# V's matmuls directly behind the scores, ahead of the transposes of q and k, in the attention slots of an attention and cosine-gated FFN kernel

## The chip, the cores and the metric

The kernel runs on one core of a Trainium2 chip. The metric is the device time of one execution in microseconds (us); less is better. TensorE does matmuls and transposes, VectorE, ScalarE and GpSimd the elementwise work, and SyncE issues the DMAs. Each engine works through its own queue of instructions; semaphores hold an instruction until what it reads is there or the buffer that it writes is free.

## What is computed

Attention with a bias that a small network makes out of the distance of two positions, and then a feed-forward layer with a cosine gate. Sizes: 4 batches, 8 heads, 576 positions, 64 dimensions a head; 2304 tokens of 512, hidden layer of 2048.

```python
def _attn_ref(q, k, v, w1, b1, w2):
    B, H, S, D = q.shape
    scale = 1.0 / np.sqrt(D)
    scores = scale * np.matmul(q, k.transpose(0, 1, 3, 2))
    ...
    h = np.maximum(x @ w1 + b1, 0.0)
    bias = h @ w2
    scores = scores + bias.transpose(2, 0, 1)[None, :, :, :]
    scores = scores - np.max(scores, axis=-1, keepdims=True)
    attn = np.exp(scores)
    attn = attn / (np.sum(attn, axis=-1, keepdims=True) + 1e-09)
    return np.matmul(attn, v).astype(np.float32)

def _moe_ref(x, w_in, w_out):
    h = x @ w_in
    g = h * np.cos(h)
    return (g @ w_out).astype(np.float32)
```

## The kernel before

Three stages follow one another: the bias tables (to about 65 us), attention (to about 370 us), and the feed-forward layer. The change touches attention alone.

A *unit* is a pair of heads of one batch; there are 16 units. The 576 rows of q are taken in five tiles: four of 128 rows, of two heads each, and a fifth that holds the last 64 rows of both heads. One tile of one unit is a *job*, and each job has a *slot*; a unit has five slots, `j` = 0 to 4, called the first to the fifth slot here. `slot(i)` writes the program out by hand, and the order in which it calls its parts is the order in which each engine gets its instructions; no scheduler moves them. A slot works on several jobs at a time:

- `qk`: the scores of the job now, on TensorE (`s`, L406), and on VectorE the bias and the row minimum (`P` and `m`, L419), which free the scores' bank. There are two buffers for `s`, one per head.
- `softmax_exp`: the exponential of the last job, one per head, on ScalarE (L437), with its sum into `dn`.
- `turn`: the transposes of the next unit's q and k on TensorE (L191, L208), a part in each of the first four slots and none in the fifth (`T_EARLY`), each followed by a copy on ScalarE (`kN`, `qT`, L198; L211 and L213 for the rest).
- `pv`: V's matmuls of the last unit (L524), in four of the five slots (`PV_EARLY`). A half of the rows is done in two slots: in the first slot of each pair chunks 0 and 1 (8 matmul instructions in the trace), in the second chunks 2 to 4 (12), and then ScalarE copies the sum into `xT` (L479, `act_copy`). So the copy into `xT` stands in the second and in the fifth slot.
- `ptrans`, `ptrans_left`: the transposes of P of the job three back (L466, L471), with copies into `PT` by ScalarE for head 0 (L479) and by VectorE for head 1 (L482), and into `PX` by VectorE (L482). All transposes share three banks (`pt`).
- `recip` and `norm`: on VectorE the step on `dn` (L449) and the reciprocal (L452), ahead of that slot's copies into `PT` and `PX`; then the normalisation of P on GpSimd (L459), in whose queue the splits of q and k (L176, L179) stand behind it.

The first slot's V matmuls read what the fifth slot just before put into `PT`; the fourth slot's read what the third put there.

```python
        T_EARLY = [["kh"], ["kl"], ["kx", "qh"], ["ql"], []]
        PV_EARLY = [[(-1, 0, (0, 1))], [(-1, 0, (2, 3, 4))], [], [(-1, 1, (0, 1))], [(-1, 1, (2, 3, 4))]]
```

In slots of every second unit VectorE and ScalarE also widen weights for the next stage (`W_PLAN`, L99 to L107).

Of the kernel before, what the change touches and what calls it, by code (L numbers as in the profile page):

```python
# [28 lines left out]
def kernel(  # L29
# [42 lines left out]
    NU = len(units)  # L72
# [38 lines left out]
    with tc.manual_schedule():  # L111
# [76 lines left out]
        def turn_main(u, x, a):  # L188
            ps = bank(F32R)
            for c in range(4):  # L190
                nc.tensor.transpose(ps[:, 128 * c : 128 * c + 128], spl[u, x][:, a, c], identr)  # L191
            if x == "q":
                o = qTs[u % 2][:, a]
            else:
                if u not in kN:
                    kN[u] = tp.tile([128, 2, 640], F32R, tag="kN", name="kN")
                o = kN[u][:, a, 64:576]
            nc.scalar.activation(  # L198
                out=o.rearrange("p (x c) -> p x c", c=4),
                in_=f(ps).rearrange("p (c x) -> p x c", c=4),  # L200
                func=AF.Copy,
                scale=-0.125 if x == "q" else 1.0,
            )

        def turn_left(u):
            ps = bank(F32R)
            for a in range(2):
                nc.tensor.transpose(ps[:, 128 * a : 128 * a + 128], spl[u, "k"][:, a, 4], identr)  # L208
            i = f(ps)[:, 0:256].rearrange("p (a x) -> p a x", a=2)
            for o in (576, 0):  # L210
                nc.scalar.activation(out=kN[u][:, :, o : o + 64], in_=i[:, :, 0:64], func=AF.Copy)  # L211
            for r in (slice(0, 64), slice(64, 128)):
                nc.scalar.activation(out=qDs[u % 2][r, :, r], in_=i[r, :, 64:128], func=AF.Copy, scale=-0.125)  # L213

        def turn(u, ops):
            if u >= NU:
                return
            for op in ops:
                if op == "kx":
                    turn_left(u)  # L220
                else:
                    turn_main(u, op[0], "hl".index(op[1]))
# [168 lines left out]
        def alloc_half(u, hf):  # L391
            PT[u, hf] = ptp.tile([128, 2, 4, WQ[hf]], F32, tag=f"h{hf}", name=f"PT{hf}")
            PX[u, hf] = px.tile([128, WQ[hf]], F32, tag=f"x{hf}", name=f"PX{hf}")
# [3 lines left out]
        def qk(u, j):  # L397
            t = tiles[j]
            heads = range(2 if t < 4 else 1)
            s = [ps_s.tile([128, 2, 512], F32, tag="s", name="s") for h in heads]  # L400
            for hf in range(2):
                for n, (a, b) in enumerate(((0, 0), (0, 1), (1, 0))):
                    for h in heads:
                        r = slice(64 * h, 64 * h + 64) if t < 4 else slice(0, 128)
                        o = HALF * hf + (64 if h == 0 else 0)
                        nc.tensor.matmul(  # L406
                            s[h][:, hf, 0:HALF],
                            qTs[u % 2][r, a, 128 * t : 128 * t + 128] if t < 4 else qDs[u % 2][:, a],
                            kN[u][r, b, o : o + HALF],
                            start=(n == 0),  # L410
                            stop=(n == 2),
                            tile_position=(r.start, 0),
                        )
            hp = units[u][0]
            P[u, j] = pp.tile([128, 1152], F32, tag="p", name="P")
            for h in heads:
                neg = P[u, j][:, 576 * h : 576 * h + 576]
                m = sv.tile([128, 2], F32, tag=f"m{h}", name="m")
                nc.vector.tensor_tensor_reduce(  # L419
                    neg.rearrange("p (a x) -> p a x", a=2),  # L420
                    s[h][:, :, 0:HALF],
                    bias[hp, t, h].rearrange("p (a x) -> p a x", a=2),
                    1.0,
                    3.0e38,
                    ALU.add,
                    ALU.min,
                    m[:, 0:1],
                )
                cur[u, j, h] = (neg, m)
# [3 lines left out]
        def softmax_exp(u, j, h):  # L433
            neg, m = cur.pop((u, j, h))
            if h == 0:
                dn[u, j] = sv.tile([128, 2], F32, tag="dn", name="dn")
            nc.scalar.activation(  # L437
                out=P[u, j][:, 576 * h : 576 * h + 576],
                in_=neg,
                func=AF.Exp,  # L440
                bias=m[:, 0:1],
                scale=-1.0,
                accum_out=dn[u, j][:, h : h + 1],
            )
# [33 lines left out]
        def act_copy(o, i):  # L478
            nc.scalar.activation(out=o, in_=i, func=AF.Copy)  # L479
# [34 lines left out]
        def pv(u, hf, chunks):  # L514
            hp, b = units[u]
            n = vN[u % 2]
            if 0 in chunks:
                X_[u, hf] = ps_v.tile([128, 512], F32, tag="v", name="pv")
            ps = X_[u, hf]
            for c in chunks:  # L520
                for h in range(2):
                    r = slice(0, 128) if c < 4 else slice(64 * h, 64 * h + 64)
                    a, m = n[r, 4 * h + c if c < 4 else 8], PT[u, hf][:, h, c, :] if c < 4 else PX[u, hf][r]
                    nc.tensor.matmul(  # L524
                        ps[64 * h : 64 * h + 64, 0 : WQ[hf]],
                        a,
                        m,
                        start=(c == 0),
                        stop=(c == 4),
                        tile_position=(r.start, 64 * h),  # L530
                        skip_group_check=True,
                    )
            if 4 in chunks:
                c0 = b * S + 256 * hf
                act_copy(xT[:, hp, c0 : c0 + WQ[hf]], X_.pop((u, hf))[:, 0 : WQ[hf]])
# [10 lines left out]
        PV_EARLY = [[(-1, 0, (0, 1))], [(-1, 0, (2, 3, 4))], [], [(-1, 1, (0, 1))], [(-1, 1, (2, 3, 4))]]  # L546
# [4 lines left out]
        def slot(i):  # L551
            u, j = divmod(i, 5)
            now, last, prev = get(i), get(i - 1), get(i - 3)
            heads = lambda x: range(2 if tiles[x[1]] < 4 else 1)
            if now:
                qk(u, j)
            if last:
                softmax_exp(*last, 0)
            turn(u + 1, T_EARLY[j])
            if last and len(heads(last)) == 2:  # L560
                softmax_exp(*last, 1)
            for du, hf, chunks in PV_EARLY[j]:
                if 0 <= u + du < NU:
                    pv(u + du, hf, chunks)
            if prev:
                if prev[1] in (0, 2):
                    alloc_half(prev[0], prev[1] // 2)
                pt = [ptrans(*prev, h) for h in heads(prev)]
                pl = ptrans_left(*prev)
            if last:  # L570
                recip(*last, 0)
                recip(*last, 1)
            if prev:
                if len(pt) == 2:
                    keep_main(*prev, 0, pt[0])
                    keep_main(*prev, 1, pt[1])
                else:
                    keep_both(prev[0], pt[0])
            if last:
                for h in heads(last):  # L580
                    norm(*last, h)
            if prev:
                keep_left(*prev, pl)
            if now:
                for du, x, step in POOL_PLAN[j]:
                    if u + du < NU:
                        split(u + du, x, step)
                for du, x in LOAD_PLAN[j]:
                    if u + du < NU:
                        load(u + du, x)  # L590
                hp, b = units[u]
                if b == B - 1 and hp + 1 < HP:
                    load_bias(hp + 1, tiles[j])
                if u == NU - 1 and j < KD:
                    split_x(0, 0, j)
                for step, at in W_PLAN:
                    w, r = divmod(i - 0 - at, 10)
                    if r == 0 and 0 <= w < len(wparts):
                        if step == "load":
                            if w + 2 < len(wparts):  # L600
                                load_w(*wparts[w + 2])
                        elif step == "abs":
                            abs_w(*wparts[w])
                        else:
                            widen_w(*wparts[w], step)
# [226 lines left out]
```

## Time and profile before

| | |
|---|---|
| median of 3 runs | 783.94 us (783.48 to 785.31) |
| profiled execution | 785.39 us, of which the profile's span is 783.6 us |
| TensorE busy | 755.1 us, 96% of the span |
| VectorE, ScalarE, GpSimd busy | 599.4, 465.4 and 395.3 us (76%, 59%, 50%) |
| TensorE's mean granted clock | 0.982 of full speed |

Busy shares are means over stages with different limits. Times below are counted from the span's start. A matmul's end is modelled in the profile, and the next one can start before it; where things follow one another without a pause, the distance of two starts is the surer measure.

### The profile page before, as it was taken

To read this page: it belongs to the slowest core of one execution; us is meant where nothing else is said; L and a number is where in the kernel's file an instruction comes from. 1 tells how busy PE (TensorE), PEld (TensorE's weight loads), DVE (VectorE), ACT (ScalarE), POOL (GpSimd) and SP (SyncE) were. 2 spreads that over 40 slices of the span, in tenths; PEclk is the share of its full clock that TensorE was granted. 3 is DMA by queue.
4 is the path that set the end of the run, shared out by engine and by line. 5 is a ranking of instruction groups with operands and counts; after the bars stand their busy time and mean duration, and the time that the engine had idled before them with its cause. 6 is when DMAs were issued, how large, how long until landed. Compare 5 with 4: busy or idle time off the path is not lost.

```text
span 783.6 us, 14808 instructions
## 1 busy us (share of the span) xinstructions
PE 755.1 (96%) x5338; PEld 603.7 (77%) x5338; DVE 599.4 (76%) x1309; ACT 465.4 (59%) x964; POOL 395.3 (50%) x486
## 2 busy tenths in 40 slices
PE   6988899999999999998999999999999999999997
PEld 2665676667666667666798989988888889899895
DVE  8973768687777777775468878899889898976655
ACT  5975677777777777785355555545454545443332
POOL 2201566676767666657345537455455464554400
PEclk9995899999999999999999999999999999999999
DMA  5775314422533161120010101111110101001112
GB/s 184 249 253 188 98 48 135 121 78 56 166 91 89 49 191 49 28 61 11 1 54 28 55 28 54 32 50 31 50 53 30 54 27 55 2 28 41 54 41 81
DMA packets 58825, 58.57 MB, mean 75 GB/s; under 512 B 28544, under 2 KB 45056, under 8 KB 58752
## 3 DMA queue, kind: packets, MB, share of 16 engines
q1 hardware_dynamic: 58752, 57.63, 24.3%
q8 instruction: 42, 0.69, 0.4%
q14 instruction: 31, 0.25, 0.1%
HBM read 42.00 MB, written 15.61 MB: 74 GB/s over the span
## 4 chain that ended last, share of the span: by engine, by line
PE 85%; DVE 6%; DMA 4%; ACT 2%; issue 2%; SPq 0%; DVEq 0%; ACTq 0%
PE ph L634 25%; PE po L689 24%; PE pv L524 12%; PE s L406 9%; PE pt L466 8%; PE pa L323 3%; PE pt L191 3%; DMA sc<-rt 2%; DVE P L419 1%; DVE ht L307 1%; PE pt L471 1%; DMA bt<-sc 1%; DVE PT L482 1%; DVE gl L663 1%; DVE acc L712 0%
## 5 line engine op out<-in xcount | busy, mean ns | idle before, releaser
L459 POOL TENSOR_SCALAR P<-P,rc 128x576 f32<-128x576 f32 x144 | 107.3, 756 | 112.7 <-ACT P L437 40.5
L638 ACT ACTIVATE a<-ph,quarter 128x384 int32<-128x384 f32 x96 | 55.6, 580 | 107.8 <-PE ph L634 107.0
L419 DVE CUSTOM_DVE_ANT_0 P<-s,bt 128x576 f32<-128x576 f32 x144 | 103.5, 751 | 20.6 <-PE s L406 13.7
L644 DVE SCALAR_TENSOR_TENSOR r<-a,ph 128x384 f32<-128x384 int32 x96 | 52.8, 550 | 79.5 <-ACT a L638 79.4
L437 ACT ACTIVATE P<-P,m 128x576 f32<-128x576 f32 x144 | 110.8, 771 | 2.6 <-DVE m L419 2.6
L509 POOL TENSOR_TENSOR xs<-xT,xs 128x384 fp32r<-128x384 f32 x96 | 107.2, 1116 | 8.0
L634 PE MATMUL ph<-xs,wpre 128*128 128x384 f32 x576 | 109.4, 338 | 0.8 <-DVE a L653 0.8
L634 PE MATMUL ph<-xs,w 128*128 128x384 f32 x576 | 108.3, 337 | 0.5 <-DVE a L653 0.5
L634 PEld LDWEIGHTS ph<-xs,wpre 128*128 128x128 f32 x576 | 101.8, 188 | 6.5 <-DVE a L653 2.1
L634 PEld LDWEIGHTS ph<-xs,w 128*128 128x128 f32 x576 | 101.4, 188 | 5.5 <-DVE a L653 1.4
L649 ACT ACTIVATE r<-r,hpi 128x384 f32<-128x384 f32 x96 | 59.3, 617 | 69.6 <-DVE r L645 69.6
L508 POOL TENSOR_SCALAR xs<-xT 128x384 fp32r<-128x384 f32 x96 | 61.6, 641 | 48.7 <-PE ph L634 48.7
L466 PEld LDWEIGHTS pt<-ident,P 128*128 128x128 f32 x576 | 62.9, 143 | 29.7 <-POOL P L459 13.7
L466 PE MATMUL pt<-ident,P 128*128 128x128 f32 x576 | 81.5, 283 | 2.3 <-DVE PT L482 2.3
L524 PE MATMUL pv<-PT,vN 128*64 128x320 f32 (+1 forms) x512 | 77.8, 424 | 2.6 <-ACT PT L479 2.4
L406 PE MATMUL s<-kN,qT 64*128 64x288 f32 x768 | 77.0, 323 | 2.8 <-DVE m L419 1.4
L689 PE MATMUL po<-w,gh 128*128 128x512 f32 x288 | 75.3, 396 | 0.0
L689 PE MATMUL po<-wpre,gh 128*128 128x512 f32 x288 | 75.2, 396 | 0.0
L663 DVE TENSOR_TENSOR gl<-a,gh 128x384 fp32r<-128x384 f32 x96 | 74.0, 771 | 0.6 <-ACT gh L657 0.6
L406 PEld LDWEIGHTS s<-kN,qT 64*128 64x128 f32 x768 | 59.0, 195 | 15.6 <-issue 7.5
L482 DVE COPY PT<-pt 128x512 f32<-128x512 f32 x64 | 43.9, 686 | 33.5 <-PE pt L466 33.5
L109 POOL TENSOR_TENSOR w<-wb,w 128x512 fp32r<-128x512 f32 x16 | 20.7, 1295 | 89.9 <-ACT w L107 89.9
(82 smaller groups left out, 1300.6 us busy)
## 6 DMA issues: line engine op xcount, KB each, us to landing
sc<-rt SPq DMA_DIRECT2D x36, 295.5 KB
raw<-in_moe_w_in_dram SPq DMA_DIRECT2D x16, 512.0 KB
raw<-in_moe_w_out_dram SPq DMA_DIRECT2D x16, 512.0 KB
bt<-sc SPq DMA_DIRECT2D x16, 288.0 KB
nk<-in_k_dram SPq DMA_DIRECT2D x16, 256.0 KB
nq<-in_q_dram SPq DMA_DIRECT2D x16, 256.0 KB
vN<-in_v_dram SPq DMA_DIRECT2D x32, 128.0 KB
bt<-sc SPq DMA_DIRECT2D x16, 256.0 KB
```

The lines of the kernel that those rows point to most:

```text
L406: nc.tensor.matmul(s[h][:, hf, 0:HALF], qTs[u % 2][r, a, 128 * t : 128 * t + 128] if t < 4 else qDs[u % 2][:, a], kN[u][r, b, o : o + HALF ...
L419: nc.vector.tensor_tensor_reduce(neg.rearrange("p (a x) -> p a x", a=2), s[h][:, :, 0:HALF], bias[hp, t, h].rearrange("p (a x) -> p a x", ...
L437: nc.scalar.activation(out=P[u, j][:, 576 * h : 576 * h + 576], in_=neg, func=AF.Exp, bias=m[:, 0:1], scale=-1.0, accum_out=dn[u, j][:, h ...
L459: nc.gpsimd.tensor_scalar(p, p, r, 1.0, ALU.mult, ALU.mult)
L466: nc.tensor.transpose(ps[:, 128 * c : 128 * c + 128], p[:, o : o + 128], ident)
L508: nc.gpsimd.tensor_scalar(h, src, 1.0, 1.0, ALU.mult, ALU.mult)
L509: nc.gpsimd.tensor_tensor(l, src, f(h), ALU.subtract)
L524: nc.tensor.matmul(ps[64 * h : 64 * h + 64, 0 : WQ[hf]], a, m, start=(c == 0), stop=(c == 4), tile_position=(r.start, 64 * h), skip_group_ ...
L634: nc.tensor.matmul(ps, a, x, start=(i == 0), stop=(i == 3 * KD - 1))
L649: nc.scalar.activation(out=r, in_=r, func=AF.Sin, scale=SIN_SCALE, bias=hpi)
L663: nc.vector.tensor_tensor(gl, a, f(G[key][0]), ALU.subtract)
L689: nc.tensor.matmul(O[n][i], a[:, 128 * i : 128 * i + 128], w, start=(i0 == 0 and p == 0), stop=(i0 == GF - 1 and p == 2),)
```

## The change

In `slot` the loop that calls `pv` moves up, from behind the second `softmax_exp` to ahead of `turn`:

```diff
             if last:
                 softmax_exp(*last, 0)
+            for du, hf, chunks in PV_EARLY[j]:
+                if 0 <= u + du < NU:
+                    pv(u + du, hf, chunks)
             turn(u + 1, T_EARLY[j])
             if last and len(heads(last)) == 2:
                 softmax_exp(*last, 1)
-            for du, hf, chunks in PV_EARLY[j]:
-                if 0 <= u + du < NU:
-                    pv(u + du, hf, chunks)
             if prev:
```

On TensorE, the second slot of a unit before (scores, transposes of k, V's matmuls on `PT` and `PX`, transposes of P, the next scores):

```order
L406 MATMUL s<-kN,qT_108 128x288 x12
L191 MATMUL pt<-identr,sk 128x128 x4
L524 MATMUL pv<-PT_1281,vN_115 64x256 x4
L524 MATMUL pv<-PX_1282,vN_115 64x256 x2
L466 MATMUL pt<-ident,P 128x128 x8
L471 MATMUL pt<-ident,P 128x128
```

The same place now:

```order
L406 MATMUL s<-kN,qT_108 128x288 x12
L524 MATMUL pv<-PT_1281,vN_115 64x256 x4
L524 MATMUL pv<-PX_1282,vN_115 64x256 x2
L191 MATMUL pt<-identr,sk 128x128 x4
L466 MATMUL pt<-ident,P 128x128 x8
L471 MATMUL pt<-ident,P 128x128
```

V's six rows of the program (12 in the trace) went ahead of the four transposes of k, which now stand with those of P. On ScalarE, the second slot of a unit, before with - and now with + (L437 is the exponential, `kN` the copy of the transposes of k, `xT` that of V's sum, `PT` that of P's transposes):

```order
 L479 ACTIVATE PT_1377<-pt 128x4x128
 L437 ACTIVATE P,dn<-P,m 128x576
-L198 ACTIVATE kN<-pt 128x512
-L437 ACTIVATE P,dn<-P,m 128x576
-L479 ACTIVATE xT<-pv 128x256
+L479 ACTIVATE xT<-pv 128x256
+L198 ACTIVATE kN<-pt 128x512
+L437 ACTIVATE P,dn<-P,m 128x576
 L479 ACTIVATE PT_1377<-pt 128x4x128
 L437 ACTIVATE P,dn<-P,m 128x576
```

The copy into `xT` went ahead of the copy into `kN` and of head 1's exponential. On ScalarE, the fifth slot, where nothing moves on TensorE:

```order
 L437 ACTIVATE P,dn<-P,m 128x576
 L479 ACTIVATE PT_1555<-pt 128x4x128
-L437 ACTIVATE P,dn<-P,m 128x576 x2
-L479 ACTIVATE xT<-pv 128x320
+L437 ACTIVATE P,dn<-P,m 128x576
+L479 ACTIVATE xT<-pv 128x320
+L437 ACTIVATE P,dn<-P,m 128x576
 L479 ACTIVATE PT_1555<-pt 128x4x128
 L437 ACTIVATE P,dn<-P,m 128x576
```

The copy into `xT` went in between the two exponentials of a job. The orders on VectorE, GpSimd and SyncE are as before.

## Rows read from the trace of the kernel before

**Rows 1.** Busy time by engine, 118 to 350 us; the columns' names first.

```profile
core 0: us, PE busy (x) PEld busy (x) DVE busy (x) ACT busy (x) POOL busy (x), PEclk, DMA share, GB/s
118.00:350.00 232.00, 229.34 (x1938) 160.26 (x1938) 175.66 (x509) 176.81 (x427) 154.90 (x208) 1.00 0.33 93
```

**Rows 2.** Waits from 99 to 372 us: total us, times, longest us.

```profile
ACT xT L479 <- PE pv L524: 18.1, 29, 1.1
...
PEld pt L471 <- ACT qD L213: 5.1, 13, 0.4
...
PEld s L406 <- DVE m L419: 3.6, 8, 1.1
```

**Rows 3.** Timeline of TensorE, last unit: start, duration, engine, line, operation.

```profile
341.69 1.05 PE L406 MATMUL s<-kN,qT 64*128 64x288 f32 x12
342.67 1.08 PE L524 MATMUL pv<-PT,vN 128*64 128x256 f32 x8
```

**Rows 4.** Timeline of TensorE, 264 to 302 us: the unit from 268.25, and the next.

```profile
271.85 1.06 PE L406 MATMUL s<-kN,qT 64*128 64x288 f32 x12
272.84 0.54 PE L191 MATMUL pt<-identr,sk 128*128 128x128 f32 x4
273.31 1.08 PE L524 MATMUL pv<-PT,vN 128*64 128x256 f32 x8
...
274.91 1.09 PE L466 MATMUL pt<-ident,P 128*128 128x128 f32 x8
...
278.62 1.58 PE L406 MATMUL s<-kN,qT 64*128 64x288 f32 x12
...
283.76 1.30 PE L524 MATMUL pv<-PT,vN 128*64 128x320 f32 x8
...
286.80 1.05 PE L406 MATMUL s<-kN,qT 64*128 64x288 f32 x12
...
298.28 0.54 PE L191 MATMUL pt<-identr,sq 128*128 128x128 f32 x4
```

**Rows 5.** Timeline of ScalarE, 264 to 302 us; idle time before and releaser in brackets.

```profile
273.42 0.60 ACT L198 ACTIVATE kN<-pt 128x512 fp32r<-128x512 f32 x1 [0.60 <-PE pt L191]
273.91 0.77 ACT L437 ACTIVATE P<-P,m 128x576 f32<-128x576 f32 x1
...
275.05 0.38 ACT L479 ACTIVATE xT<-pv 128x256 f32<-128x256 f32 x1 [0.28 <-PE pv L524]
275.60 0.60 ACT L479 ACTIVATE PT<-pt 128x512 f32<-128x512 f32 x1 [0.17 <-PE pt L466]
...
277.43 0.45 ACT L211 ACTIVATE kN<-pt 128x128 fp32r<-128x128 f32 x2 [0.48 <-PE pt L208]
...
283.08 0.77 ACT L437 ACTIVATE P<-P,m 128x576 f32<-128x576 f32 x1
...
283.84 0.76 ACT L437 ACTIVATE P<-P,m 128x576 f32<-128x576 f32 x1
...
285.81 0.44 ACT L479 ACTIVATE xT<-pv 128x320 f32<-128x320 f32 x1 [1.11 <-PE pv L524]
...
298.14 0.58 ACT L479 ACTIVATE PT<-pt 128x512 f32<-128x512 f32 x1
```

**Rows 6.** Timeline of VectorE, 264 to 285 us.

```profile
264.64 0.17 DVE L449 TENSOR_SCALAR dn<-dn 128x2 f32<-128x2 f32 x1 [0.90 <-ACT P L437]
...
264.92 0.67 DVE L482 COPY PT<-pt 128x512 f32<-128x512 f32 x1
...
274.80 0.53 DVE L449 TENSOR_SCALAR dn<-dn 128x2 f32<-128x2 f32 x1
...
276.04 0.69 DVE L482 COPY PT<-pt 128x512 f32<-128x512 f32 x1 [0.50 <-PE pt L466]
...
278.34 0.75 DVE L419 CUSTOM_DVE_ANT_0 P<-s,bt 128x576 f32<-128x576 f32 x1
```

**Rows 7.** Timeline of VectorE and of TensorE's weight loads (PEld), first slot's place behind the last unit.

```profile
358.95 0.69 DVE L482 COPY PT<-pt 128x512 f32<-128x512 f32 x1 [1.47 <-PE pt L466]
...
359.69 0.62 PEld L524 LDWEIGHTS pv<-PT,vN 128*64 128x64 f32 x6 [0.34 <-DVE PT L482]
```

**Rows 8.** Timeline of GpSimd, 264 to 285 us.

```profile
273.90 1.42 POOL L179 TENSOR_TENSOR sq<-nq,sq 128x256 fp32r<-128x256 f32 x2
```

**Rows 9.** Busy time of two units in a row, 268.25 to 304.98 us: the sum's line.

```profile
sum 36.73, PE 36.28 PEld 25.41 DVE 27.67 ACT 28.14 POOL 24.69; mean PE 18.14 PEld 12.70 DVE 13.83 ACT 14.07 POOL 12.34
```

## The prediction

> **What bounds the kernel now.** I first took the busy times of the attention stage alone. From 118 to 350 us TensorE is busy 229.34 of 232 us, at a granted clock of 1.00, which is the 2.4 GHz level, while ScalarE has 176.81, VectorE 175.66 and GpSimd 154.90 [rows 1]. So the reader is to see a stage whose time is TensorE's, and in which the other engines have a quarter of their time left. A change of order on TensorE that leaves its work alone can only give or take waits. Next I read who waits for whom. TensorE's own waits in this stage are few: the 13 for the copies into qD (5.1 us in all) and the 8 for VectorE's reductions of the scores (3.6 us). ScalarE on the other hand sits 29 times, 18.1 us in all, until V's matmuls are done, for its copy into xT [rows 2]. Last I read the timeline of one unit, engine by engine, to see what stands behind that copy.
>
> **TensorE's own work.** In four of a unit's five slots V's matmuls exist; in three of these (first, second, fourth) the four transposes of q or k now stand behind V's and not ahead of them. No matmul is added or removed. What the new neighbours cost can be read: in the last unit there are no transposes of q or k, so V's matmuls already stand directly behind the scores. Scores take 0.98 us there from start to V's start (341.69 to 342.67) [rows 3], against 0.99 from scores to the transposes (271.85 to 272.84) [rows 4]. V's matmuls take 1.60 us to the start of the transposes of P (273.31 to 274.91), with the weight change behind them; the transposes of k take 0.47 (272.84 to 273.31) [rows 4]. I take 1.60 for V to the transposes of k too, since both kinds of transposes load full 128 by 128 weights. So P's transposes would begin at the same time as before, and this term is nothing, unless the weight change costs differently. The bounds: the 0.01 us above, 45 times, is 0.5 us either way.
>
> **ScalarE's order is where it costs.** The copy into xT belongs to V's block, so it moves as well, in the second and in the fifth slot: from behind the exponential of head 1 to ahead of it (in the second slot also ahead of the copy into kN). ScalarE works in order, so that exponential now waits for V's matmuls. Behind the exponential come, on ScalarE, the copy of head 0 into PT, and on VectorE, which waits for the exponential's sum, the step on dn, the reciprocal and the copy of head 1 into PT.
>
> *Fifth slot into the first of the next unit.* TensorE's order is unchanged in the fifth slot (no transposes of q or k there), so xT starts where it did, at 285.81, 2.05 us after V's start at 283.76 [rows 4, 5]. ScalarE begins an instruction 0.11 us before the end of a copy ahead of it (273.42 plus 0.60, and the next at 273.91), so the exponential starts at 285.81 + 0.44 - 0.11 = 286.14 instead of 283.84: 2.30 us late [rows 5]. From the start of an exponential to dn it is 0.89 us (273.91 to 274.80), from dn to the copy of head 1 0.28 (264.64 to 264.92), the copy takes 0.69 [rows 5, 6], and V's second matmul starts 0.05 after such a copy (358.95 + 0.69, then 359.69) [rows 7]. That is 286.14 + 0.89 + 0.28 + 0.69 + 0.05 = 288.05. V's matmuls of the first slot read this copy. Directly behind the scores they could start at 286.80 + 0.98 = 287.78. The transposes of k, which stood between and covered this, are behind them now. Wait: **0.27 us**.
>
> *Second slot.* V's matmuls start at 272.84, where the transposes stood. xT starts 1.74 us after V's start (273.31 to 275.05), at 274.58, and leaves ScalarE at 274.85. The transposes of k start at 272.84 + 1.60 = 274.44, their copy 0.58 later (272.84 to 273.42), at 275.02; the exponential 0.49 after that, at 275.51 instead of 273.91: 1.60 late. An exponential holds ScalarE 0.76 (283.08 to 283.84), so the copy of head 0 starts at 276.27 instead of 275.60: 0.67 late. On VectorE dn starts at 275.51 + 0.89 = 276.40, and the copy of head 1 at 276.68 instead of 276.04: 0.64 late [rows 4 to 6].
>
> *What that reaches.* There are two kinds of units by turns. In the one, VectorE widens weights in the third slot and works without a pause from the copy at 276.04 to the reduction at 278.34, which frees the bank that the fourth slot's scores wait for: those take 1.58 us instead of 1.06 [rows 4, 6]. All of the 0.64 reaches TensorE: **0.64 us**. In the other kind VectorE has no such work and takes up most of the lateness; there ScalarE decides. In the third slot ScalarE had 0.58 us of slack ahead of the two copies into kN (275.60 + 0.49 + 0.76 = 276.85, start at 277.43), so 0.09 of the 0.67 is left. The copy of the fifth tile into PT then starts at 298.14 + 0.09 and is done 0.58 later, and V's matmuls start 0.05 after that, at 298.86; directly behind the scores they could have started at 298.28 [rows 4, 5]. Wait: **0.58 us**. Here too it was the transposes of q that covered the copy.
>
> **Sum.** A unit costs 0.27 + (0.64 + 0.58) / 2 = 0.88 us more. V's matmuls run in 15 of the units' rounds plus a tail that I count as part of the last: 15 x 0.88 = 13.2 us. Nothing behind gives it back: the next stage is TensorE's as well. The profiled execution took 785.39 us, 1.45 above the median of 783.94; 785.39 + 13.2 = 798.6, and on the median's scale **797.1 us**.
>
> **A price that the walk leaves out.** I took 0.17 us for dn, from dn to the reciprocal. One row shows 0.53: the dn at 274.80 ended at 275.33, as GpSimd's two subtractions for q (273.90 plus 1.42) ended at 275.32 [rows 6, 8]. If the later dn met such work in both places, a unit would cost 2 x 0.36 = 0.72 more. I take nothing: in the second slot dn moves to 276.40, past that work, and in the fifth GpSimd's next instructions are normalisations that themselves wait for this dn's reciprocal. The Trainium skill (SBUF — State Buffer, "Who interferes with whom") says that a VectorE scalar operation in a two-port mode and a GpSimd instruction shut each other out for the whole instruction. By that rule the trace agrees (0.53 against 0.17), and the sum would be 13.2 where they miss each other and 24.0 where they meet.
>
> **The rivals.**
> Hidden, no change (about 784): the exponential is late, but ends in idle time. ScalarE and VectorE have a quarter of the stage free [rows 1], which speaks for it. It is decided in the first and fourth slots: V's matmuls would have to find both copies into PT done when the scores end, so the chain would have to be 0.27 and 0.58 us shorter than the rows make it. I see no such slack. This also covers the case that the new order does nothing since TensorE has no gap between scores and V.
> Faster: the early xT lets ScalarE run ahead, and TensorE's waits for qD and for the reductions vanish: 5.1 + 3.6 = 8.7 us [rows 2], 775. Against it: the copy of head 0 at 275.60 was held by TensorE's transposes (0.17 idle), not by xT [rows 5]. It turns to this side only if that copy starts before 275.60.
> Slower still: dn meets GpSimd's work, as above: 785.39 + 24.0, on the median's scale 807.9. That needs GpSimd's subtractions to slide along with VectorE.
>
> **How the numbers follow.** Forecast 0.83, hidden 0.06, faster 0.04, slower still 0.07. A measurement of this kernel tells about 0.2%, 1.6 us, from no change. Slower holds forecast and last rival, 0.90; same 0.06; faster 0.04. For the range: if the first slot's wait is hidden and the fourth's is half, 15 x 0.30 = 4.5 us, 788.4; the top is where dn meets GpSimd both times, 807.9. Range 788 to 808.
>
> **What will show it.** The exponential of head 1 directly behind xT in the second and fifth slots, about 1.6 and 2.3 us later than now; V's matmuls waiting for PT by VectorE in the first slot and by ScalarE in every second unit's fourth; longer waits of the scores for m in the units between; two units in a row, 36.73 us now [rows 9], at about 36.73 + 1.76 = 38.5. TensorE's busy gaps from V to the transposes of k should be as those from V to P's transposes. If these gaps are larger, or the copies into PT are on time when the scores end, I am wrong.

## The result and the profile after

The changed kernel takes 792.24 us in the median (791.61 to 793.57, 4 runs) against 783.71 us beside it: a ratio of 1.011, 95% interval 1.0087 to 1.0132. It is 8.5 us slower; 13.2 us slower had been forecast. The profiled execution took 792.06 us, its span is 790.3 us.

The two units of the windows that answer to [rows 9], columns as in [rows 1]:

```profile
253.13:271.86 18.73, 18.23 (x155) 12.87 (x155) 11.82 (x39) 13.79 (x35) 11.51 (x16) 1.00 0.18 49
271.86:290.95 19.09, 18.35 (x154) 12.87 (x154) 13.18 (x41) 13.73 (x35) 13.62 (x17) 1.00 0.56 152
sum 37.82, PE 36.58 PEld 25.74 DVE 25.00 ACT 27.52 POOL 25.12; mean PE 18.29 PEld 12.87 DVE 12.50 ACT 13.76 POOL 12.56
```

Two units take 37.82 us instead of 36.73: 0.55 us more a unit, at the same granted clock of 1.00. Fifteen times 0.55 is 8.2 us, so nearly all of the loss sits in the steady units. The waits after, from 99 to 372 us, as [rows 2] of before and two groups more:

```profile
DVE dn L449 <- ACT P L437: 75.2, 55, 2.3
ACT xT L479 <- PE pv L524: 42.9, 29, 1.8
...
PEld s L406 <- DVE m L419: 7.2, 14, 1.2
...
PEld pv L524 <- ACT PT L479: 4.4, 8, 0.9
```

ScalarE now sits 42.9 us ahead of its copies into xT (18.1 before), VectorE sits 75.2 us until an exponential's sum is there, and TensorE waits for reductions 14 times and not 8, and 8 times for ScalarE's copy into PT (2 before). Where that arises is seen in ScalarE's timeline of a second slot (its scores start at 275.60) and a fifth:

```profile
278.33 0.39 ACT L479 ACTIVATE xT<-pv 128x256 f32<-128x256 f32 x1 [1.77 <-PE pv L524]
278.76 0.60 ACT L198 ACTIVATE kN<-pt 128x512 fp32r<-128x512 f32 x1
279.25 0.77 ACT L437 ACTIVATE P<-P,m 128x576 f32<-128x576 f32 x1
...
280.01 0.59 ACT L479 ACTIVATE PT<-pt 128x512 f32<-128x512 f32 x1
...
289.96 0.44 ACT L479 ACTIVATE xT<-pv 128x320 f32<-128x320 f32 x1 [1.17 <-PE pv L524]
290.29 0.77 ACT L437 ACTIVATE P<-P,m 128x576 f32<-128x576 f32 x1
```

Head 1's exponential starts 3.65 us after the second slot's scores, where it started 2.06 after them [rows 4, 5], with ScalarE idle for 1.77 us ahead of the copy that was put in front of it. In the fifth slot it stands right behind xT. VectorE's timeline of that second slot and of the third:

```profile
280.14 0.17 DVE L449 TENSOR_SCALAR dn<-dn 128x2 f32<-128x2 f32 x1 [1.60 <-ACT P L437]
...
280.43 0.67 DVE L482 COPY PT<-pt 128x512 f32<-128x512 f32 x1
...
282.60 0.75 DVE L419 CUSTOM_DVE_ANT_0 P<-s,bt 128x576 f32<-128x576 f32 x1
```

The copy of head 1 stands 4.83 us after the scores instead of 4.19, and the reduction that frees the scores' bank is late with it. TensorE's timeline, the units from 253.13 and from 271.86:

```profile
263.70 1.33 PE L406 MATMUL s<-kN,qT 64*128 64x288 f32 x12
265.30 1.30 PE L524 MATMUL pv<-PT,vN 128*64 128x320 f32 x8 [0.27 <-ACT PT L479]
...
272.84 1.34 PE L524 MATMUL pv<-PT,vN 128*64 128x256 f32 x8
...
276.60 1.08 PE L524 MATMUL pv<-PT,vN 128*64 128x256 f32 x8
...
278.19 0.53 PE L191 MATMUL pt<-identr,sk 128*128 128x128 f32 x4
278.56 1.06 PE L466 MATMUL pt<-ident,P 128*128 128x128 f32 x8
...
281.25 0.51 PE L191 MATMUL pt<-identr,sq 128*128 128x128 f32 x4 [0.23 <-DVE PT L482]
...
282.73 0.39 PE L406 MATMUL s<-kN,qT 64*128 64x288 f32 x1 [0.23 <-DVE m L419]
283.41 1.06 PE L406 MATMUL s<-kN,qT 64*128 64x288 f32 x11 [0.28 <-DVE m L419]
```

Four waits: V's matmuls of a first slot are stretched to 1.34 us, as against 1.08 in a second slot; in the third slot of either kind of unit the transposes of q wait 0.23 us for VectorE's late copy into PT, which gives back their bank; in the one kind of unit V waits in the fourth slot for PT; in the other the fourth slot's scores wait for the reduction. And one gain: the transposes of P start 0.37 us after those of k (278.19 to 278.56), where V started 0.47 after them [rows 4].

### The profile page after: what moved, and what is told of

Its sections match the earlier page's. It is cut to its first block, busy times and chain, and to the rows that moved or that the text cites. A ratio compares the mean times of both kernels' runs of the same rounds, so it can differ in the third digit from the quotient of the medians.

```text
span 790.3 us, 14822 instructions
## 1 busy us (share of the span) xinstructions
PE 755.6 (96%) x5338; PEld 606.6 (77%) x5338; DVE 582.9 (74%) x1309; ACT 461.1 (58%) x964; POOL 399.5 (51%) x486
## 4 chain that ended last, share of the span: by engine, by line
PE 83%; DVE 7%; ACT 6%; DMA 2%; issue 1%; SPq 0%; DVEq 0%; ACTq 0%
PE ph L634 25%; PE po L689 24%; PE pv L524 13%; PE s L406 8%; PE pt L466 7%; PE pa L323 3%; PE pt L191 3%; ACT P L437 2%; DMA sc<-rt 2%; DVE P L419 2%; DVE ht L307 1%; ACT PT L479 1%; PE pt L471 1%; DVE wb L105 1%; ACT kN L198 1%
## 5 line engine op out<-in xcount | busy, mean ns | idle before, releaser
L459 POOL TENSOR_SCALAR P<-P,rc 128x576 f32<-128x576 f32 x144 | 112.3, 791 | 129.3 <-ACT PT L479 86.7
L437 ACT ACTIVATE P<-P,m 128x576 f32<-128x576 f32 x144 | 110.9, 770 | 3.2 <-DVE m L419 3.2
L524 PE MATMUL pv<-PT,vN 128*64 128x320 f32 (+1 forms) x512 | 82.3, 428 | 5.0 <-ACT PT L479 5.0
L406 PE MATMUL s<-kN,qT 64*128 64x288 f32 x768 | 76.4, 318 | 6.2 <-DVE m L419 5.9
L689 PE MATMUL po<-wpre,gh 128*128 128x512 f32 x288 | 75.2, 396 | 0.0
L449 DVE TENSOR_SCALAR dn<-dn 128x2 f32<-128x2 f32 (+1 forms) x80 | 14.9, 186 | 80.9 <-ACT P L437 80.8
L406 PEld LDWEIGHTS s<-kN,qT 64*128 64x128 f32 x768 | 58.0, 190 | 18.6 <-DVE m L419 10.2
```

The lines of the kernel that those rows point to most:

```text
L406: nc.tensor.matmul(s[h][:, hf, 0:HALF], qTs[u % 2][r, a, 128 * t : 128 * t + 128] if t < 4 else qDs[u % 2][:, a], kN[u][r, b, o : o + HALF ...
L437: nc.scalar.activation(out=P[u, j][:, 576 * h : 576 * h + 576], in_=neg, func=AF.Exp, bias=m[:, 0:1], scale=-1.0, accum_out=dn[u, j][:, h ...
L459: nc.gpsimd.tensor_scalar(p, p, r, 1.0, ALU.mult, ALU.mult)
L524: nc.tensor.matmul(ps[64 * h : 64 * h + 64, 0 : WQ[hf]], a, m, start=(c == 0), stop=(c == 4), tile_position=(r.start, 64 * h), skip_group_ ...
L689: nc.tensor.matmul(O[n][i], a[:, 128 * i : 128 * i + 128], w, start=(i0 == 0 and p == 0), stop=(i0 == GF - 1 and p == 2),)
```

## Slot by slot

From the starts of the scores' first weight loads (their line is L406, in kernels with rewritten helpers L414) the length of each slot can be taken. In the steady units it repeats within 0.03 us, which tells more than the whole time, where the start of the attention stage alone differs by up to 2.7 us from profile to profile (first scores at 62.47 to 65.14 us). Where the two kinds of units differ, the unit in whose first three slots VectorE widens no weight stands first; it is called the unit without widening.

| kernel | first | second | third | fourth | fifth | unit |
|---|---|---|---|---|---|---|
| before | 3.60 | 4.19 | 2.59 | 3.76 / 4.15 | 4.03 | 18.18 / 18.55 |
| changed | 3.75 | 4.06 | 2.76 / 3.06 | 4.11 / 4.17 | 4.05 | 18.73 / 19.09 |
| 1 ScalarE's order alone | 3.60 | 4.39 | 2.75 / 3.05 | 3.90 / 4.29 | 4.03 | 18.68 / 19.36 |
| 2 TensorE's order alone | 3.49 | 4.06 | 3.03 / 3.06 | 4.10 / 4.17 | 4.05 | 18.72 / 18.83 |
| 3 exponentials first | 3.49 | 4.06 | 2.76 | 3.50 / 3.96 | 4.05 | 17.86 / 18.32 |
| 4 as 3, fourth slot old | 3.49 | 4.06 | 2.76 | 3.62 / 3.95 | 4.03 | 17.97 / 18.29 |
| 5 as 3, TensorE old | 3.60 | 4.39 | 2.75 | 3.62 | 4.03 | 18.39 |
| 6 fifth slot's exponential back | 3.49 | 4.06 | 2.76 / 3.06 | 4.10 / 4.18 | 4.05 | 18.47 / 18.83 |
| 7 second slot's exponential back | 3.74 | 4.06 | 2.57 / 2.69 | 4.11 / 4.17 | 4.05 | 18.54 / 18.70 |
| 8 as 3, third slot mixed | 3.49 | 4.06 | 2.58 | 4.32 / 4.26 | 4.10 | 18.55 / 18.50 |
| 9 changed, widening later | 4.06 / 3.75 | 4.06 | 2.76 | 4.11 | 4.05 | 19.04 / 18.73 |
| 10 as 3, widening later | 3.49 | 4.06 | 2.76 | 3.49 | 4.05 | 17.85 |
| 11 as 9, subtraction later | 3.75 | 4.06 | 2.76 | 4.11 | 4.05 | 18.73 |

## The experiments

The theory: TensorE's new order is harmless or better, and the loss comes from the copy into xT in ScalarE's queue, which makes head 1's exponential late. The rival: TensorE's order itself is the loss, since V directly behind the scores finds its operands not ready. To part the two, `turn` and `pv` were split into their matmuls and their copies: `ts()` and `vs()` issue the matmuls and give the copies back, `do` issues these, `exp1()` is head 1's exponential. In these terms the changed kernel is:

```python
            v = vs()
            t = ts()
            do(v)
            do(t)
            exp1()
```

Before, it was `t = ts()`, `do(t)`, `exp1()`, `v = vs()`, `do(v)`. Times are medians, each beside runs of the kernel before on the same chip.

**1. ScalarE's order alone.**

```diff
-            v = vs()
             t = ts()
+            v = vs()
             do(v)
             do(t)
             exp1()
```

> TensorE keeps the order of the kernel before (transposes of q and k, then V), and ScalarE takes the order of the changed kernel (copy into xT, copies of the transposes, exponential of head 1). Theory, ScalarE's order is the loss: in the second slot the exponential comes 1.9 us late, the copies into PT 0.4 to 0.9 us; the fifth slot's lateness is covered by the transposes that still stand ahead of V. About 0.67 us a unit, 15 units: 10 us slower than before (8 to 13). Rival, TensorE's order is the loss (V directly behind the scores finds its operands not ready): no change, within 1.5 us of before.

793.02 us against 783.47, ratio 1.0116 (1.0096 to 1.0136): 9.6 us slower, with TensorE's order untouched. The rival falls. The first slot is as before (3.60), so the transposes of k do cover the fifth slot's lateness. In the second slot 0.2 us was lost that I had not foreseen: TensorE waits there for the late copy into kN to give back its bank (13 times, 2.7 us of idle weight loads in all).

**2. TensorE's order alone.**

```diff
             v = vs()
             t = ts()
-            do(v)
             do(t)
             exp1()
+            do(v)
```

> TensorE takes the order of the changed kernel (V, then transposes of q and k), and ScalarE keeps the order of before (copies of the transposes, exponential of head 1, copy into xT). Theory, ScalarE's order is the loss and TensorE's new order in itself saves 0.13 us in each of three slots: the first slot's wait of 0.27 goes, the second slot's exponential stays 1.6 us late since the transposes of k come later. 0.27 us a unit less than the changed kernel: about 4 us slower than before (0 to 6). Rival, TensorE's order is the loss: 8 to 9 us slower, as the changed kernel.

789.80 us against 783.47, ratio 1.0073 (1.0052 to 1.0094): 6.3 us slower, just above the theory's span of 0 to 6 and below the rival's 8 to 9. The first slot's wait is gone as foretold (3.49). But the exponential still stands behind the copy of k, whose transposes come late, and xT now stands behind both, so that the copies behind them come later still: the third slot, where TensorE waits for the copies into PT and qD, is 3.03 us in the units without widening instead of 2.76.

**3. Both exponentials first.**

```diff
             v = vs()
             t = ts()
+            exp1()
             do(v)
             do(t)
-            exp1()
```

> TensorE in the order of the changed kernel; ScalarE does both exponentials of a job first in every slot, then xT, then the copies of the transposes. Theory: no exponential is late, so the waits for PT in the first and fourth slots and the late reductions go, and the 0.13 us in each of three slots (0.39 us a unit) stays as a gain, less up to 0.2 us a unit for the third slot's copies of k: 3 to 6 us faster than before. Rival, TensorE's order is the loss: still 5 to 9 us slower than before.

779.22 us against 783.47, ratio 0.9941 (0.9922 to 0.9961): 4.3 us *faster* than before, with TensorE's order that of the changed kernel. So that order is no loss: the first, second and fourth slots are 0.11 to 0.26 us shorter than before, and only the third is 0.17 longer.

**4. The same, fourth slot in the old order on TensorE.**

```diff
-            v = vs()
-            t = ts()
+            if j == 3:
+                t = ts()
+                v = vs()
+            else:
+                v = vs()
+                t = ts()
             exp1()
```

> As the one with both exponentials first, but in the fourth slot the transposes of q stay ahead of V's matmuls. Theory: 0.13 us a unit less of the gain of TensorE's order, and the fourth slot's wait for PT is covered: 2 to 4 us faster than before, and within 2 us of the one with all slots in the new order. Rival, V finds PT late in the fourth slot whatever ScalarE does: this one is over 4 us faster than that one.

779.88 us, ratio 0.9958 (0.9943 to 0.9974), 0.7 us apart from the run before it in the medians. With the exponentials first, V finds PT in time in the fourth slot, and the old order there costs 0.12 us in the units without widening (3.62 against 3.50). In the others nothing of that is seen (3.95 against 3.96): there the fourth slot's scores are stretched in both kernels, to 1.39 us here and 1.53 in experiment 3.

**5. Exponentials first, TensorE as before.**

```diff
-            v = vs()
             t = ts()
+            v = vs()
             exp1()
             do(v)
             do(t)
```

> TensorE in the order of before, ScalarE with both exponentials first as in the third experiment. Theory, the gain of that experiment is TensorE's (0.13 us in each of three slots, since the transposes of q, k and P stand together): it is gone here, 4 to 6 us slower than the third experiment, so within 2 us of the kernel before. Rival, the gain is ScalarE's, by earlier exponentials: as fast as the third experiment, 4 us faster than before.

783.97 us against 782.90, ratio 1.0014 (0.9994 to 1.0035): the gain is gone, as the theory had it, so it was not ScalarE's alone. The slots are not as clean as the time. In the units without widening the first and the fourth show TensorE's 0.11 and 0.12 us (3.60 and 3.62 against 3.49 and 3.50). The second, at 4.39, has the wait for kN's bank on top, as in experiment 1. In the units with widening the fourth goes the other way (3.62 against 3.96): VectorE's step ahead of the reduction (L105) takes 0.68 us here and 1.02 in experiment 3.

**6. The changed kernel, fifth slot's exponential ahead again.**

```diff
-            do(v)
-            do(t)
-            exp1()
+            if j == 4:
+                exp1()
+                do(v)
+            else:
+                do(v)
+                do(t)
+                exp1()
```

> The changed kernel with one thing undone: in the fifth slot head 1's exponential stands ahead of the copy into xT again. Theory: the first slot's wait for the copy of head 1 into PT goes, 0.27 us a unit, 4 us faster than the changed kernel (3 to 5). Rival, the fifth slot's lateness is hidden and the second slot makes all of the loss: as the changed kernel, within 1.5 us.

790.30 us against 782.90, ratio 1.0094 (1.0071 to 1.0117). The first slot falls from 3.75 to 3.49 in every unit and nothing else moves: the wait is where it was put, at 0.25 us. The whole time fell only from 1.011 to 1.0094 of before, about 1.3 us and not the 3 to 5 expected, with intervals that overlap widely. In the profiled execution twelve steady units are 3.1 us shorter than in the changed kernel's (223.8 against 226.9), but the span only 2.3. Some of it was given back in the last unit's fourth slot, 5.44 us instead of 3.86, where the granted clock was 0.62 and not 1.00 (most of the stretch at the lower level):

```profile
355.65 2.40 PE L532 MATMUL pv<-PT,vN 128*64 128x320 f32 x8
356.00:360.00 4.00, 4.00 (x21) 2.50 (x18) 2.38 (x8) 0.81 (x2) 3.92 (x5) 0.62 0.04 15
```

V's matmuls took 1.30 us at this place in the changed kernel. TensorE had waited 1.01 and 0.28 us for reductions just before, and in the changed kernel, where the clock stayed, 1.00 and 0.28. So why it fell is open, and whether it fell in the other executions is not shown.

**7. The changed kernel, second slot's exponential ahead.**

```diff
-            do(v)
-            do(t)
-            exp1()
+            if j == 1:
+                exp1()
+                do(v)
+                do(t)
+            else:
+                do(v)
+                do(t)
+                exp1()
```

> The changed kernel with one thing undone: in the second slot head 1's exponential stands ahead of the copies into xT and kN. Theory: the 0.6 us a unit of the third and fourth slots go but for the fourth slot's wait for PT in every second unit (0.49); first slot 0.27 - 0.39 of TensorE's gain + 0.25 = 0.13 us a unit more than before: about 2 us slower than before (0 to 4), 6 to 7 faster than the changed kernel. Rival, the fifth slot makes the loss: as the changed kernel.

787.22 us against 782.90, ratio 1.0055 (1.0033 to 1.0077), 4.3 us slower than before: about 4 us of the changed kernel's loss is gone, less than the 6 to 7 expected. The third slot recovers (2.57 and 2.69), but the fourth stays at 4.11 and 4.17. In the units without widening V waits there for PT, as I had counted on. In the others it is still the reduction that the scores wait for, which I had not:

```profile
278.10 1.17 DVE L105 SCALAR_TENSOR_TENSOR wb<-raw,wb 128x512 uint32<-128x512 uint32 x1
...
279.87 0.75 DVE L427 CUSTOM_DVE_ANT_0 P<-s,bt 128x576 f32<-128x576 f32 x1
```

```profile
280.68 1.05 PE L414 MATMUL s<-kN,qT 64*128 64x288 f32 x11 [0.28 <-DVE m L427]
```

The copy into PT ahead is no longer late, but the widening step behind it takes 1.17 us, as against 0.78 in the changed kernel and 0.90 in the kernel before, so the reduction stays late.

**8. Exponentials first, but the third slot's kN and qD ahead of them.**

```diff
-            exp1()
-            do(v)
-            do(t)
+            if j == 2:
+                do(t[:1])
+                exp1()
+                do(t[1:])
+            else:
+                exp1()
+                do(v)
+                do(t)
```

> The third experiment's kernel, but in the third slot the copies of the last rows of k and q (kN, qD) stand ahead of head 1's exponential, and the copy into qT behind it. There TensorE waits 0.34 us for the qD copies in each unit, as against 0.16 before. Theory: the wait falls back by 0.18 us a unit: 2 to 3 us faster than the third experiment. Rival: the time goes into the next wait, the copy of the fifth tile into PT or the reductions: no change, within 1 us.

784.92 us against 782.90, ratio 1.0029 (1.0012 to 1.0046): some 6 us slower than experiment 3, where the theory wanted 2 to 3 faster. The third slot did fall, from 2.76 to 2.58, but the fourth rose from 3.50 to 4.32. The rows of this kernel, ScalarE's copy into PT and TensorE's V behind it (the third slot starts at 256.74):

```profile
258.13 0.45 ACT L217 ACTIVATE kN<-pt 128x128 fp32r<-128x128 f32 x2 [0.47 <-PE pt L212]
...
260.43 0.59 ACT L487 ACTIVATE PT<-pt 128x512 f32<-128x512 f32 x1
```

```profile
261.07 1.30 PE L532 MATMUL pv<-PT,vN 128*64 128x320 f32 x8 [0.57 <-ACT PT L487]
```

In experiment 3 the exponential fills the 0.47 us in which ScalarE waits for the transposes of k. Here this idle time is back, the copy into PT starts 3.69 us after the slot's scores instead of 2.96 (275.01 after 272.05 there), and V waits for it. The rival's place was right, and the price was far above "no change".

**9. The changed kernel, a widening step later.**

```diff
-        W_PLAN = [("abs", 2), (0, 3), (0.5, 4), (1, 5), (2, 6), ("load", 6), (3, 7), (4, 7)]
+        W_PLAN = [("abs", 2), (0, 3), (0.5, 4), (1, 5), (2, 7), ("load", 7), (3, 8), (4, 8)]
```

> The changed kernel, with the third step of widening a weight (VectorE, 0.8 us, between the copies of the second slot and the reductions of the third in every second unit) one slot later, and what follows it one slot later too. Theory: in those units it is what makes the reductions late for the fourth slot's scores (third slot 3.06 us as against 2.76 in the others); without it these units take as long as the others, 18.73 instead of 19.09 us: 0.36 us in 7 units, 2 to 3 us faster than the changed kernel. Rival, those scores wait for the late copies alone, with or without widening: no change.

790.92 us against 782.82, ratio 1.0102 (1.0089 to 1.0115), where the changed kernel has 1.011: less than 1 us faster, and not the 2 to 3 expected. The third slot is 2.76 in all units, so VectorE's widening was the reason for 3.06, and the units with widening take 18.73 us, as expected. But the first slot of the units behind them rose to 4.06, and those take 19.04. GpSimd's, VectorE's and TensorE's rows there:

```profile
291.60 1.28 POOL L109 TENSOR_TENSOR wpre<-wb,wpre 128x512 fp32r<-128x512 f32 x1
292.41 0.50 DVE L449 TENSOR_SCALAR dn<-dn 128x2 f32<-128x2 f32 x1 [1.77 <-ACT P L437]
293.02 0.67 DVE L482 COPY PT<-pt 128x512 f32<-128x512 f32 x1
...
293.16 1.67 PE L524 MATMUL pv<-PT,vN 128*64 128x256 f32 x8
```

The step on dn took 0.50 us and not 0.17; it ended at 292.91, as GpSimd's subtraction did at 292.88. V, which waits for the copy behind it, is stretched from 1.34 to 1.67. This is the price that the prediction left out of the sum, met in another kernel.

**10. Exponentials first, with the same step later.** The edit of experiment 9 in the kernel of experiment 3.

> The kernel with both exponentials first (third experiment), with the same widening step one slot later. Theory: every second unit's fourth slot falls from 3.96 to 3.50 us, 0.46 us in 7 units: 3 us faster than the third experiment, about 1% faster than before. Rival: the step only moves the wait into the fifth slot's reductions: no change.

774.97 us against 782.82, ratio 0.9900 (0.9882 to 0.9918): 7.9 us faster than before, the fastest of all. The unit is 17.85 us in both kinds; the fifth slot stays at 4.05, so the rival falls.

**11. The changed kernel, with GpSimd's subtraction behind the normalisations.**

```diff
-        W_PLAN = [("abs", 2), (0, 3), (0.5, 4), (1, 5), (2, 7), ("load", 7), (3, 8), (4, 8)]
+        W_PLAN = [("abs", 2), (0, 3), (0.5, 4), (1, 5), (2, 7), ("load", 7), (3, 8), (4, 9)]
```

> As the run with the widening step one slot later, but GpSimd's subtraction of the widened weight (1.28 us) one slot later still, behind the normalisations of the fifth slot. In that run the first slot of every second unit took 4.06 us and not 3.75, and its step on dn 0.50 us and not 0.17. Theory, VectorE's step on dn had to wait for GpSimd's subtraction: the first slot is 3.75 us in all units, dn 0.17, 0.31 us in 7 units, about 2 us faster than that run. Rival, ScalarE's widening copy in the fourth slot made the fifth slot's exponential late: the first slot stays at 4.06.

788.63 us against 782.52, ratio 1.0081 (1.0061 to 1.0101), as against 1.0102 in experiment 9. These intervals overlap, so it is the slots that tell: the first is 3.75 in all units, and the step on dn of the place in question takes 0.17 again:

```profile
287.57 0.17 DVE L449 TENSOR_SCALAR dn<-dn 128x2 f32<-128x2 f32 x1 [1.77 <-ACT P L437]
```

It still comes as late (1.77 us of waiting ahead of it in both), so not the exponential but GpSimd's subtraction had made it long.

## Why the prediction was right, and where its size was off

**ScalarE's order: right, step by step.** In the second slot I had put xT 1.74 us after V's start, and it stands at 1.73 (276.60 to 278.33). The exponential, the copy of head 0, dn and the copy of head 1 were put at 3.66, 4.42, 4.55 and 4.83 us after the scores; they stand at 3.65, 4.41, 4.54 and 4.83. That this order makes a loss with TensorE's untouched is shown by experiment 1. Its 9.6 us are not the same waits one by one: they hold 0.20 us a unit for kN's bank, which the changed kernel does not lose, and not the first slot's wait.

**The first slot's wait: right.** 0.27 us forecast; V is stretched by 0.26, and experiment 6 takes 0.25 off by undoing the fifth slot alone.

**Third and fourth slots: right in sum, not in every place.** Forecast 0.64 in units with widening and 0.58 in the others. Third and fourth slot together grew by 0.49 and 0.52 us in the table, and with the 0.12 that TensorE's order saves in the fourth (below) the waits are 0.61 and 0.64. The reasons given are shown too: by experiment 9 (without the widening the third slot is 2.76 in all units) and by V's wait for PT in the rows after. What I had not seen is the bank: in the units without widening 0.17 us is lost in the third slot already, where the transposes of q wait for VectorE's late copy, and V's own wait in the fourth slot is 0.27 us and not 0.58. And in units with widening V's wait stands right behind that of the scores: experiment 9 took the scores' away, TensorE then waited for ScalarE's copy into PT 14 times instead of 8, and those units became 0.36 us shorter, not 0.64.

**TensorE's own work: this is the term that was mis-sized.** I had written that "P's transposes would begin at the same time as before, and this term is nothing", with bounds of 0.5 us. It measures 0.11 us in the first slot (3.60 to 3.49, experiments 5 and 3), 0.13 in the second (4.19 to 4.06, before and after) and 0.12 in the fourth (units without widening of experiments 3, 4 and 5): some 0.35 us a unit, 5.3 us in 15 units, to the good. I had priced the change of weights from V to the transposes of k rightly (1.59 us from 276.60 to 278.19, forecast 1.60), but forgotten that the change from those transposes to V goes away as well: V started 0.47 after them, and P's transposes start 0.37 after them. The trace of before had the row for it, in the third slot, where transposes of P follow those of q without V in between:

```profile
277.23 0.51 PE L191 MATMUL pt<-identr,sq 128*128 128x128 f32 x4
277.58 0.63 PE L466 MATMUL pt<-ident,P 128*128 128x128 f32 x4
```

That is 0.35 us. With this term, 15 x (0.88 - 0.35) = 8.0 us, against 8.5 measured. About 0.10 us of each slot's gain is this border; the other 0.01 to 0.03 was not followed.

That 792.24 lies within 788 to 808 owes something to luck. The range's lower end was reasoned from waits that would be hidden, and none was. What brought the result so low in the range is TensorE's term, which came out at ten times its bound.

**The rivals.** Hidden: no, both waits stand at their places. Faster: the copy of head 0 starts later and not earlier, as was held against it. Its 8.7 us were also too much: they are idle time of the weight loads, and the matmuls themselves stood idle at these places for 2.1 and 1.1 us. Slower still, by dn behind GpSimd's work: it did not happen in the changed kernel, where dn takes 0.17 in these places, but it did in experiment 9, at 0.33 us, and experiment 11 undid it. The prediction named one such row of before; there are longer ones in the same trace:

```profile
282.72 1.01 DVE L449 TENSOR_SCALAR dn<-dn 128x2 f32<-128x2 f32 x1 [0.80 <-ACT P L437]
```

```profile
282.40 1.30 POOL L109 TENSOR_TENSOR wpre<-wb,wpre 128x512 fp32r<-128x512 f32 x1
```

They did not reach TensorE there, whose only wait for VectorE's copy into PT from 99 to 372 us is 0.3 us of idle weight loading. In the changed kernel every dn from 118 to 350 us takes 0.14 to 0.17.

The Trainium skill (SBUF — State Buffer, "Who interferes with whom") says that a VectorE scalar operation in a two-port mode and a GpSimd instruction shut each other out for the whole instruction. The trace of experiment 9 agrees: 0.50 against 0.17 us, ending within 0.03 us of GpSimd's instruction.

## What to carry to other kernels

A block that is moved takes along the copies that it issues on other engines, and their place in those queues can cost more than the block's own place gains: here TensorE's new order is worth some 5 us, and ScalarE's, that came with it, costs some 13 (15 units of 0.26 and 0.61 or 0.64 us). Put what starts a long chain (the exponential) ahead of what only drains a result, and move matmuls and their copies separately. When TensorE's blocks change places, count the change of weights at every border that appears and at every one that goes away.

## What was not expected of the hardware

Four transposes of q or k cost TensorE 0.46 to 0.51 us from start to start with V's 64-column weights behind them, most often 0.47, and 0.34 to 0.38 with the transposes of P behind them. The border between transposes and V thus costs about 0.1 us, besides the 0.38 to 0.49 us of idle weight loading that stood behind V in both kernels. What in it costs this time (the shape of the weights, the type, or the place in the array) was not tried.
